# Attention's probabilities transposed in 32x32 blocks on VectorE and regrouped by DMA, in place of TensorE transposes

## The chip, the cores and the metric

The kernel runs on one core of one Trainium2 chip. The metric is the device time of one execution in microseconds (us), as the median of several runs. TensorE (PE, with its weight loads PEld), VectorE (DVE), ScalarE (ACT), GpSimd (POOL) and the DMA queue of SyncE (SP) run side by side, each through its own instructions in a fixed order, and wait for each other by semaphores.

## The reference

All of it is fp32. Three stages follow each other:

```
chunked attention: q, k, v (8 batches, 8 heads, 576, 64), chunks of 64
  s = (q_c @ k_c^T) / 8 ;  p = exp(s - max(s)) / (sum + 1e-9) ;  o = p @ v_c
  x = o as (4608 tokens, 512)
cos layer:   h = x @ w_in (512x2048) ;  y = (h * cos(h)) @ w_out (2048x512)
SoLU layer:  h2 = y @ w_in2 (512x1024) ;  z = h2 * softmax(h2)
             out = layernorm(z) * g_ln @ w_out2 (1024x512)
```

## The kernel before, in words

The large products are done as three matmuls on split operands (high by high, high by low, low by high), 128x512 each. Tokens go in 9 tiles of 512. The first part of the program is a row of 144 steps, 16 for each tile: step n does twelve matmuls `h` (`mm_in`, the first product, lines 533 to 535), ScalarE and VectorE make h*cos(h) out of it and split it into `gh` and `gl`, and two steps later twelve matmuls `y` (`mm_out`, lines 600 to 602) add it into the second product. The SoLU layer follows, tile by tile of 128 tokens (`h2` and `o`).

Attention is done in 20 units, numbered from 0. Units 0 to 3 hold 128 tokens each and run ahead of the steps. Units 4 and 5 hold 256 tokens, are loaded in natural order and have operands that step over 8 elements (`natural`). Units 6 to 19 hold 256 tokens as well (two units to a tile of 512); they are the 14 units that the change touches. The table `wide` spreads the work of such a unit over eight steps: q and k transposed in 32x32 blocks on VectorE (`att_tr`), 32 small matmuls 64x64 for the scores `sc` (`att_qk`), maximum, subtraction, exponential, sum and division (`att_max` to `att_mul`, tile `p`), then in step 5 `att_pt`: eight 128x128 transposes of `p` on TensorE into the PSUM tile `pt`. In step 6 `att_ptc` copies `pt` to SBUF on ScalarE (tile `ptb`), `att_pv` does 32 small matmuls with v (PSUM tile `x`), and in step 7 `att_x` splits `x` on ScalarE and VectorE into `xh` and `xl`, from which the `h` matmuls of that tile of 512 tokens read. The first step that reads both units of tile j is step 16j: step 32 for units 6 and 7, step 48 for units 8 and 9, and so on.

The PSUM tiles `sc`, `pt` and `x` of these units share one buffer (tag `a`), and `qt`, `kt`, `p`, `ptb` share two SBUF buffers (tag `t`, `work`). Many helpers show as line 105, so rows are told apart by tile.

A scheduler sets the order of each engine's instructions when the program is built: it takes what it believes ready, by priority of the place in the program. Calls through `pe`, `act`, `dve` are held to program order only ahead of the steps; within the steps matmuls of different tiles can be placed among each other. The chip then runs the order as it is. All loads and most stores are issued by SP, one after the other; a load or store whose condition isn't met holds back those behind it. There are eight DMA semaphores taken in turn, and a DMA waits for the one eight places before it.

Of the kernel before, what the change touches and what calls it, by code (L numbers as in the profile page):

```python
# [29 lines left out]
def kernel(  # L30
# [12 lines left out]
    nc = tc.nc  # L43
# [5 lines left out]
    CH = 64  # L49
# [107 lines left out]
    def wtile(dt, name, n=1024):  # L157
        return wp.tile([P, n], dt, tag="w", name=name)
# [103 lines left out]
    UNITS = [(2 * i, 2) for i in range(SUB)] + [(c, 4) for c in range(8, NT // CH, 4)]  # L262
    NU = len(UNITS)
    HU = H // 2


    NAT = SUB + 2
    GA = 8

    def small(i):  # L270
        return i < SUB

    def work(i, shape, tag, name):

        if small(i) or (i == SUB + 1 and tag != "t"):
            t = wtile(F32, name, 512 if small(i) else 1024)
        else:
            t = ap_.tile([P, 1024], F32, tag=tag, name=name, bufs=2 if tag == "t" else 1)
        letters = "abcde"[:len(shape)]
        sizes = {x: n for x, n in zip(letters, shape)}  # L280
        return t.rearrange(f"p ({' '.join(letters)}) -> p {' '.join(letters)}", **sizes)
# [17 lines left out]
    v0 = su.tile([P, HU, 2 * SUB, D], F32, name="v0")  # L299
# [96 lines left out]
    def natural(i, ap):  # L396
        return ap.rearrange("p (a g) -> p g a", a=GA) if SUB <= i < NAT else ap
# [58 lines left out]
    pt, ptb = {}, {}  # L456

    def att_pt(i):
        p = pr.pop(i)
        x = UNITS[i][1] // 2 * HU  # L460
        if small(i):
            t = ps_h.tile([P, x, P], F32, tag="h", name="pt")
        else:
            t = ps_a.tile([P, x, P], F32, tag="a", name="pt")
        for y in range(x):
            pe.transpose(out=t[:, y], in_=p[:, y].rearrange("p r k -> p (r k)"), identity=ident)
        pt[i] = t
# [8 lines left out]
    def att_pv(i):  # L476
        n = UNITS[i][1]

        t = (ps_y if small(i) else ps_a).tile([P, 2, 512], F32, tag="y" if small(i) else "a", name="x")
        a, b = vi.pop(i, None), ptb.pop(i)  # L480
        for y in range(n * HU // 2):
            for row in range(2):
                for col in range(2):
                    rs = slice(row * CH, (row + 1) * CH)
                    if small(i):
                        w, c = divmod(y, n)
                        u = 2 * w + col
                        m, p = v0[rs, u, UNITS[i][0] + c], b[rs, u, c * CH:(c + 1) * CH]
                    else:
                        u, cc = divmod(y, 2)  # L490
                        m, p = a[rs, cc, 2 * u + col], b[rs, cc * HU + u, col * CH:(col + 1) * CH]
                    pe.matmul(
                        out=t[col * CH:(col + 1) * CH, row, y * CH:(y + 1) * CH],
                        lhsT=m,
                        rhs=natural(i, p),
                        start=True,
                        stop=True,
                    )
        xps[i] = t[:, :, 0:n * HU // 2 * CH]
# [136 lines left out]
    if True:  # L636
# [23 lines left out]
        for c in range(4):  # L660
            sync.dma_start(
                out=gcol[32 * c:32 * (c + 1)],
                in_=g_ln.rearrange("(c q p) -> c p q", c=4, p=32)[c],
# [20 lines left out]
        att_mul(0)  # L684
        tok(2)
        att_pt(0)
        att_max(1)
        att_sub(1)
# [7 lines left out]
        att_mul(1)  # L696
        tok(3)
        att_pt(1)
        att_max(2)
        att_sub(2)  # L700
# [5 lines left out]
        att_sum(2)  # L706
        att_mul(2)
        att_pv(0)
        att_pt(2)
        att_max(3)  # L710
        att_sub(3)
        att_exp(3)
        att_ptc(2)
        att_pv(1)
        att_pv(2)
        att_sum(3)
        att_mul(3)
# [24 lines left out]
        def load_next_v(i):  # L742
# [3 lines left out]
        wide = (  # L746
            (0, "early", lambda i: att_tr(i, "q")), (1, "early", lambda i: att_tr(i, "k")),
            (1, "late", att_qk), (1, "late", load_next), (2, "early", att_max), (3, "early", att_sub),
            (3, "mid", att_exp), (4, "early", att_sum), (5, "early", att_mul), (5, "late", att_pt),
            (6, "early", att_ptc), (6, "late", att_pv), (6, "late", load_next_v), (7, "early", att_x),  # L750
        )
        tight = (
            (0, "early", lambda i: att_nat(i, "q")), (0, "early", lambda i: att_natc(i, "q")),
# [12 lines left out]
        for i in range(SUB, NU):  # L766
            j, o = divmod(UNITS[i][0] * CH, T)
# [111 lines left out]
        for n in range(NSTEP + LAG + 1):  # L879
# [20 lines left out]
            r = n - NB  # L900
# [8 lines left out]
            m, late_by = divmod(n - 40, 10)  # L909
# [69 lines left out]
```

## Time and profile before

| | |
|---|---|
| median of 3 runs | 1342.62 us (1342.1 to 1344.93) |
| profiled execution, its own time | 1340.4 us |
| span of the profiled execution | 1338.6 us |
| PE busy in the span | 1294.7 us (97%) |
| DVE busy | 928.0 us (69%) |
| ACT busy | 724.7 us (54%) |
| steps with attention of units 6 to 19 | about 170 to 820 us |
| mean granted TensorE clock | 0.992 |

Matmuls are pipelined: a row shows each from its start to its end, some 0.39 us for a 128x512 matmul, while the next starts 0.23 us after it. What an operation costs TensorE is read from the distance of starts.

### The profile page before, as it was taken

Reading aid. Unit: us, or ns where it says so; the run is one execution under the profiler, and the core shown is the slowest. Engines: PE = TensorE matmul, PEld = TensorE weight load, DVE = VectorE, ACT = ScalarE, POOL = GpSimd, SP = SyncE. Lnnn points to the kernel's source line nnn. Section 1 sums busy time; section 2 is a strip of 40 time slices with the busy share of each in tenths; the row PEclk is TensorE's granted clock in tenths of the full one; section 3 lists DMA queues with packets and bytes.
Section 4 is the critical chain, followed back from the end, with each engine's and each line's share of the span. In section 5 each row is a group of like instructions: output and inputs, shape, how many; then the busy total and the mean of one; then the engine's idle time right before and its main releaser. Section 6 shows DMA issues by size and latency. Waiting matters only on the chain.

```text
span 1338.6 us, 19864 instructions
## 1 busy us (share of the span) xinstructions
PE 1294.7 (97%) x7760; PEld 1035.8 (77%) x7760; DVE 928.0 (69%) x1362; ACT 724.7 (54%) x1065; POOL 23.1 (2%) x43
## 2 busy tenths in 40 slices
PE   5899999999999999999999999999799999999998
PEld 4566877888888888788888788887677888888877
DVE  4888987666786877877787776665676655666460
ACT  3877887666555556655564655455244343444241
POOL 0000000000000000000000000000000000000000
PEclk9899999999999999999999999999899999999999
DMA  8942342322431522332342300620623334333432
GB/s 244 208 101 71 118 111 64 60 78 53 111 94 29 148 50 62 97 77 57 86 94 50 117 10 14 222 79 1 190 86 102 87 87 126 87 87 79 95 73 69
DMA packets 212512, 122.98 MB, mean 92 GB/s; under 512 B 176065, under 2 KB 184257, under 8 KB 210881
## 3 DMA queue, kind: packets, MB, share of 16 engines
q1 hardware_dynamic: 212320, 121.57, 35.4%
q8 instruction: 61, 1.00, 0.3%
q14 instruction: 35, 0.28, 0.1%
q10 hardware_dynamic: 96, 0.13, 0.0%
HBM read 73.40 MB, written 29.36 MB: 77 GB/s over the span
## 4 chain that ended last, share of the span: by engine, by line
PE 83%; DVE 8%; ACT 5%; issue 1%; DMA 1%; POOL 0%; SPq 0%; DVEq 0%; ACTq 0%; POOLq 0%
PE h L533 9%; PE y L600 9%; PE y L602 9%; PE y L601 9%; PE h L535 9%; PE h L534 8%; PE o L865 5%; PE o L863 5%; PE o L864 5%; PE h L795 4%; PE h L794 4%; PE h L793 4%; DVE z L105 2%; PE x L105 2%; PE sc L105 1%
## 5 line engine op out<-in xcount | busy, mean ns | idle before, releaser
L533 PE MATMUL h<-xh,whi 128*128 128x512 f32 x576 | 232.9, 404 | 1.3 <-ACT xh L105 1.3
L534 PE MATMUL h<-xl,whi 128*128 128x512 f32 x576 | 225.7, 392 | 0.9 <-DVE xl L105 0.9
L535 PE MATMUL h<-xh,wlo 128*128 128x512 f32 x576 | 226.0, 392 | 0.1
L600 PE MATMUL y<-gh,whi 128*128 128x512 f32 x544 | 213.4, 396 | 3.9 <-ACT whi L105 2.0
L602 PE MATMUL y<-gh,wlo 128*128 128x512 f32 x544 | 214.9, 395 | 0.1
L601 PE MATMUL y<-gl,whi 128*128 128x512 f32 x544 | 214.9, 395 | 0.0
L562 ACT ACTIVATE r<-r 128x512 f32<-128x512 f32 x144 | 90.9, 631 | 177.1 <-DVE r L556 176.9
L570 DVE SCALAR_TENSOR_TENSOR hs<-r,hs 128x512 f32<-128x512 f32 x136 | 93.9, 690 | 96.2 <-ACT r L563 96.0
L105 DVE TENSOR_TENSOR gl<-hs,gh 128x512 fp32r<-128x512 f32 x136 | 93.7, 689 | 54.3 <-ACT gh L105 53.7
L105 ACT ACTIVATE gh<-hs 128x512 fp32r<-128x512 f32 x136 | 85.6, 630 | 83.2 <-DVE hs L570 76.7
L533 PEld LDWEIGHTS h<-xh,whi 128*128 128x128 f32 x576 | 108.6, 188 | 27.5 <-issue 1.6
L534 PEld LDWEIGHTS h<-xl,whi 128*128 128x128 f32 x576 | 108.7, 189 | 24.8 <-issue 1.7
L535 PEld LDWEIGHTS h<-xh,wlo 128*128 128x128 f32 x576 | 108.4, 188 | 24.4 <-issue 0.5
L600 PEld LDWEIGHTS y<-gh,whi 128*128 128x128 f32 x544 | 101.9, 188 | 29.7 <-ACT ye L610 3.5
L601 PEld LDWEIGHTS y<-gl,whi 128*128 128x128 f32 x544 | 102.1, 188 | 25.7 <-DVE gl L105 1.6
L793 PE MATMUL h<-whi,yh 128*128 128x512 f32 x288 | 113.2, 393 | 8.3 <-ACT yh L105 7.6
L602 PEld LDWEIGHTS y<-gh,wlo 128*128 128x128 f32 x544 | 102.1, 188 | 24.2 <-DVE wlo L105 0.5
L863 PE MATMUL o<-whi,lh 128*128 128x512 f32 x288 | 113.1, 393 | 3.9 <-ACT lh L105 3.9
L865 PE MATMUL o<-whi,ll 128*128 128x512 f32 x288 | 113.6, 394 | 3.1 <-DVE ll L105 2.7
L553 DVE SCALAR_TENSOR_TENSOR r<-kt,hs 128x512 f32<-128x512 int32 x144 | 99.4, 690 | 22.3 <-ACT kt L548 19.1
L794 PE MATMUL h<-wlo,yh 128*128 128x512 f32 x288 | 112.7, 391 | 0.0
L864 PE MATMUL o<-wlo,lh 128*128 128x512 f32 x288 | 112.6, 391 | 0.0
(93 smaller groups left out, 1941.2 us busy)
## 6 DMA issues: line engine op xcount, KB each, us to landing
lt<-bt SPq DMA_DIRECT2D x144, 128.0 KB
yd<-ye SPq DMA_DIRECT2D x22, 512.0 KB
yr<-yd SPq DMA_DIRECT2D x22, 512.0 KB
out<-os SPq DMA_DIRECT2D x142, 64.0 KB
vi<-in_v SPq DMA_DIRECT2D x64, 128.0 KB
qi<-in_q SPq DMA_DIRECT2D x224, 32.0 KB
ki<-in_k SPq DMA_DIRECT2D x224, 32.0 KB
st<-in_moe_w_in SPq DMA_DIRECT2D x10, 512.0 KB
```

Of the source, the lines that this page charges most:

```text
L105: ins = getattr(self.engine, name)(*args, **kwargs)
L533: nc.tensor.matmul(out=t, lhsT=wa, rhs=xh[j][:, kk, :], start=(kk == 0), stop=False)
L534: nc.tensor.matmul(out=t, lhsT=wa, rhs=xl[j][:, kk, :], start=False, stop=False)
L535: nc.tensor.matmul(out=t, lhsT=wb, rhs=xh[j][:, kk, :], start=False, stop=(kk == KD - 1))
L600: nc.tensor.matmul(out=o, lhsT=wa, rhs=a, start=head, stop=False)
L601: nc.tensor.matmul(out=o, lhsT=wa, rhs=b, start=False, stop=False)
L602: nc.tensor.matmul(out=o, lhsT=wb, rhs=a, start=False, stop=last)
L793: nc.tensor.matmul(out=ps[:, hh], lhsT=a[:, kk], rhs=whi, start=(kk == 0), stop=False)
L794: nc.tensor.matmul(out=ps[:, hh], lhsT=a[:, kk], rhs=wlo, start=False, stop=False)
L863: nc.tensor.matmul(out=o, lhsT=hi, rhs=whi, start=(f == 0), stop=False)
L864: nc.tensor.matmul(out=o, lhsT=hi, rhs=wlo, start=False, stop=False)
L865: nc.tensor.matmul(out=o, lhsT=lo, rhs=whi, start=False, stop=(f == NF2 - 1))
```

## The change

For units from `NAT` (6) on, `att_pt` issues one VectorE transpose of `p` in 32x32 blocks into a new tile `ptr`, and sixteen DMAs from SP, SBUF to SBUF, each 32 partitions of 256 elements (32 KB), which carry block (g, c) of `ptr` to partition group g of `ptb`. The TensorE transposes and the ScalarE copy of these units are gone (`att_ptc` stays for units 0 to 5). In `att_pv` the moving operand of these units is two runs of 32 elements, 256 elements apart, where it was 64 elements in a row. In `wide`, `att_mul` moves from step 5 early to step 4 late, with `att_pt` behind it; `att_pv` keeps step 6 late.

```diff
     def att_pt(i):
         p = pr.pop(i)
         x = UNITS[i][1] // 2 * HU
+        if i >= NAT:
+
+            t = work(i, (4, x, 32), "t", "ptr")
+            o = work(i, (4, x, 32), "t", "ptb")
+            tc.keep_in_program_order(
+                nc.vector.transpose(
+                    out=t.rearrange("p g x s -> p x g s"),
+                    in_=p.rearrange("p x r (h s) -> p x (r h) s", s=32),
+                )
+            )
+            for g in range(4):
+                for c in range(4):
+                    nc.sync.dma_start(
+                        out=o[32 * g:32 * (g + 1), c].rearrange("p x s -> p (x s)"),
+                        in_=t[32 * c:32 * (c + 1), g].rearrange("p x s -> p (x s)"),
+                    )
+            ptb[i] = o
+            return
         if small(i):
...
                     if small(i):
                         w, c = divmod(y, n)
                         u = 2 * w + col
-                        m, p = v0[rs, u, UNITS[i][0] + c], b[rs, u, c * CH:(c + 1) * CH]
+                        m, p = v0[rs, u, UNITS[i][0] + c], natural(i, b[rs, u, c * CH:(c + 1) * CH])
                     else:
                         u, cc = divmod(y, 2)
-                        m, p = a[rs, cc, 2 * u + col], b[rs, cc * HU + u, col * CH:(col + 1) * CH]
+                        m, x = a[rs, cc, 2 * u + col], cc * HU + u
+                        if i < NAT:
+                            p = natural(i, b[rs, x, col * CH:(col + 1) * CH])
+                        else:
+                            p = b[rs, 2 * col:2 * col + 2, x, :]
...
-                        rhs=natural(i, p),
+                        rhs=p,
...
-            (3, "mid", att_exp), (4, "early", att_sum), (5, "early", att_mul), (5, "late", att_pt),
-            (6, "early", att_ptc), (6, "late", att_pv), (6, "late", load_next_v), (7, "early", att_x),
+            (3, "mid", att_exp), (4, "early", att_sum), (4, "late", att_mul), (4, "late", att_pt),
+            (6, "late", att_pv), (6, "late", load_next_v), (7, "early", att_x),
```

The change moves instructions, since the scheduler orders anew. First place: TensorE at the product with v of unit 12, before. Its 32 matmuls (`x`) stand in one piece between the `y` of step 67 and the `h` of step 70.

```order
L601 MATMUL y_4447<-gl_4521,whi_1233 128x512
L602 MATMUL y_4447<-gh_4520,wlo_1234 128x512
L105 MATMUL x_4593<-ptb_4565,vi_4164 64x64 x32
L533 MATMUL h_4631<-xh_3734,whi_901 128x512
L534 MATMUL h_4631<-xl_3735,whi_901 128x512
```

The same unit now (its last two pieces; two more single matmuls stand further up, the first among the `h` of step 70, `h_4687`; `h_4732` is step 71):

```order
L555 MATMUL h_4732<-xh_3774,whi_901 128x512
L556 MATMUL h_4732<-xl_3775,whi_901 128x512
L105 MATMUL x_4649<-ptb_4553,vi_4212 64x64
L557 MATMUL h_4732<-xh_3774,wlo_902 128x512
L555 MATMUL h_4732<-xh_3774,whi_901 128x512
L556 MATMUL h_4732<-xl_3775,whi_901 128x512
L557 MATMUL h_4732<-xh_3774,wlo_902 128x512
L105 MATMUL x_4649<-ptb_4553,vi_4212 64x64 x29
```

The 32 matmuls are now in pieces of 1, 1, 1 and 29. Over units 6 to 19 the sizes are: 1, 1, 30 (unit 6); 1, 31 (unit 7); 1, 1, 1, 29 (units 8 to 13 and 15 to 17); 32 (units 14 and 19); 2, 1, 29 (unit 18), which is 46 pieces. Before, they were 4, 3, 2, 23 in unit 6, 5 and 27 in unit 18 and one piece in the other twelve, which is 18.

Second place: TensorE at the product with v of unit 7, now. `h_2445` is step 32, the first that reads what this unit makes (`xh_1953`, `xl_1954`); `h_2553` is step 33.

```order
L622 MATMUL y_2171<-gh_2463,whi_1820 128x512
L105 MATMUL x_2325<-ptb_2229,vi_1935 64x64
L623 MATMUL y_2171<-gl_2464,whi_1820 128x512
L624 MATMUL y_2171<-gh_2463,wlo_1821 128x512
L105 MATMUL x_2325<-ptb_2229,vi_1935 64x64 x31
L555 MATMUL h_2445<-xh_1953,whi_288 128x512
L555 MATMUL h_2553<-xh_1953,whi_288 128x512
L556 MATMUL h_2445<-xl_1954,whi_288 128x512
L557 MATMUL h_2445<-xh_1953,wlo_289 128x512
```

Before, two whole steps (48 matmuls 128x512) stood between the last `x` of unit 7 and the first `h` of step 32; now none does. In unit 17 five `y` matmuls stand between its last `x` and the first `h` of step 112; in the units 9, 11, 13 and 15 there are at least 12 large matmuls there.

Third place: VectorE behind the division of unit 12 (`p<-p,s`), before and then now. `gl_4435` and `gl_4483` are the split of step 65, `kt` and `r` belong to step 66.

```order
L105 TENSOR_TENSOR p_4429<-p_4429,s_4473 128x1024
L570 SCALAR_TENSOR_TENSOR hs_4391<-r_4394,hs_4391 128x512
L550 TENSOR_SCALAR kt_4440<-hs_4438 128x512
L553 SCALAR_TENSOR_TENSOR r_4441<-kt_4440,hs_4438 128x512
L105 TENSOR_TENSOR gl_4435<-hs_4391,gh_4434 128x512
```

```order
L105 TENSOR_TENSOR p_4477<-p_4477,s_4521 128x1024
L592 SCALAR_TENSOR_TENSOR hs_4439<-r_4442,hs_4439 128x512
L572 TENSOR_SCALAR kt_4488<-hs_4486 128x512
L466 STREAM_TRANSPOSE ptr_4552<-p_4477 128x8x4x32
L105 TENSOR_TENSOR gl_4483<-hs_4439,gh_4482 128x512
```

The new transpose stands two instructions behind the division and ahead of the split that the `y` of step 65 waits for; one `r` that stood ahead of that split is now behind it.

## Rows read from the trace of the kernel before

**Rows 1.** Page part 1: engine, busy us (share of the span), instructions.

```profile
PE 1294.7 (97%) x7760; PEld 1035.8 (77%) x7760; DVE 928.0 (69%) x1362; ACT 724.7 (54%) x1065; POOL 23.1 (2%) x43
```

**Rows 2.** Windows: us, busy of PE, PEld, DVE, ACT, POOL, PEclk, DMA share, GB/s.

```profile
440.00:480.00 40.00, 40.00 (x296) 32.48 (x295) 32.00 (x47) 23.50 (x34) 0.00 (x0) 1.00 0.46 124
```

**Rows 3.** Chain that ended last, in order of time: start us, us, what.

```profile
197.58 3.10 DMA vi<-in_v
...
448.42 1.09 PE sc L105 x64
...
471.81 0.87 PE pt L105 x8
...
478.24 1.09 PE x L105 x64
```

**Rows 4.** Groups by shape: busy us, mean ns, then idle before.

```profile
L105 PE MATMUL pt<-ident,p 128*128 128x128 f32 x144 | 20.4, 285 | 1.5 <-DVE p L105 1.5
...
L390 DVE STREAM_TRANSPOSE qt<-qi 128x1024 f32<-128x1024 f32 x14 | 17.3, 1237 | 0.0
...
L105 DVE TENSOR_TENSOR xl<-x,xh 128x1024 fp32r<-128x1024 f32 x16 | 19.6, 1224 | 3.9 <-ACT xh L105 3.9
...
L105 ACT ACTIVATE xh<-x 128x1024 fp32r<-128x1024 f32 x16 | 16.2, 1012 | 1.3 <-PE x L105 0.8 <-PE h L535 0.5
```

**Rows 5.** Timeline of PE around one whole product with v: start us, us, operation.

```profile
430.15 0.40 PE L602 MATMUL y<-gh,wlo 128*128 128x512 f32 x1
430.48 1.16 PE L105 MATMUL x<-ptb,vi 64*64 64x64 f32 x64
431.57 0.50 PE L533 MATMUL h<-xh,whi 128*128 128x512 f32 x1
431.90 0.40 PE L534 MATMUL h<-xl,whi 128*128 128x512 f32 x1
```

**Rows 6.** Timeline of PE, a piece of unit 18.

```profile
756.43 0.39 PE L535 MATMUL h<-xh,wlo 128*128 128x512 f32 x1
756.75 0.44 PE L105 MATMUL x<-ptb,vi 64*64 64x64 f32 x10
757.12 0.50 PE L600 MATMUL y<-gh,whi 128*128 128x512 f32 x1
757.46 0.39 PE L601 MATMUL y<-gl,whi 128*128 128x512 f32 x1
```

**Rows 7.** Timeline of PE, a piece of unit 6.

```profile
191.23 0.64 PE L600 MATMUL y<-gh,whi 128*128 128x512 f32 x2
191.80 0.33 PE L105 MATMUL x<-ptb,vi 64*64 64x64 f32 x4
192.06 0.50 PE L601 MATMUL y<-gl,whi 128*128 128x512 f32 x1
192.40 0.39 PE L602 MATMUL y<-gh,wlo 128*128 128x512 f32 x1
```

**Rows 8.** Timeline of PE, unit 4, whose moving operand steps over 8 elements.

```profile
69.55 2.09 PE L105 MATMUL x<-ptb,vi 64*64 64x64 f32 x64
71.58 0.50 PE L535 MATMUL h<-xh,wlo 128*128 128x512 f32 x1
```

**Rows 9.** Timeline of SP: sixteen DMAs of 32 partitions.

```profile
1074.74 10.04 SPq L847 DMA_DIRECT2D lt<-bt  x16
```

**Rows 10.** Timeline of DVE behind the division of units 12 and 13.

```profile
458.91 1.23 DVE L105 TENSOR_TENSOR p<-p,s 128x1024 f32<-128x1024 f32 x1
...
461.72 0.69 DVE L105 TENSOR_TENSOR gl<-hs,gh 128x512 fp32r<-128x512 f32 x1
...
510.39 0.68 DVE L105 TENSOR_TENSOR gl<-hs,gh 128x512 fp32r<-128x512 f32 x1
```

**Rows 11.** Timeline of PE: a wait for whi; first gl matmul behind unit 13.

```profile
215.44 0.50 PE L600 MATMUL y<-gh,whi 128*128 128x512 f32 x1 [1.99 <-ACT whi L105]
...
511.26 0.40 PE L601 MATMUL y<-gl,whi 128*128 128x512 f32 x1
```

## The prediction

> **What bounds the kernel now.** I read the page's busy times first: TensorE works 97% of the span, VectorE 69% [rows 1]. The windows then show where: in a stretch with units 11 and 12 TensorE is busy 40.00 of 40.00 us at a granted clock of 1.00, which is the upper of its two levels, 2.4 GHz, while VectorE has 8 us left and the DMA engines are under half busy [rows 2]. The chain that ended last is what the reader should look at next: in that stretch it stays on TensorE, and a unit's scores, its transposes (0.87 us) and its product with v lie on it one after the other [rows 3]. So here a microsecond taken off TensorE is a microsecond of the program, if nothing else comes late, and work added to VectorE or SP is free until TensorE waits for it. Durations of single matmuls mislead: a transpose lasts 285 ns on average [rows 4], but eight of them take 0.87 us of the chain.
>
> **What is removed.** Eight transposes of 14 units: 14 x 0.87 = 12.2 us off TensorE, all of it on the chain [rows 3]. The ScalarE copies of `pt` go too; they were hidden beside TensorE, so I give nothing for them.
> The Trainium skill's page "TensorE: Matmul & The Clock Gate", section "Part 4: PE-mode transpose", has a transpose at some 275 ns inside a kernel; the mean here agrees with that, but 14 x 8 x 0.275 would be 30.8 us by that figure, and the chain shows transposes pipelined, each starting some 0.1 us after the last. The row decides.
>
> **What the new order adds on TensorE.** The sum turns on the product with v, which the scheduler now cuts up: 46 pieces where there were 18, 28 more. What a cut costs is read from pieces that stand in the kernel before. A large matmul starts 0.23 us after the last (two together take 0.64 us, one 0.40 [rows 7]). A whole product (64 rows of the trace for 32 matmuls) stretches three starts of large matmuls from 0.46 to 431.90 - 430.15 = 1.75 us, so 1.29 us [rows 5]. A piece of 10 rows takes 757.46 - 756.43 - 0.46 = 0.57 us [rows 6]. The line through both is 13.3 ns for a row and 0.44 us for being a piece at all. A third piece tests it: 4 rows between large matmuls, 192.40 - 191.23 - 3 x 0.23 = 0.48 us, where the line gives 0.49. The fixed part is the gap on both sides (0.32 us to the first small matmul, 0.34 us from the first large one to the next) and the time in which one small matmul runs through alone. I take 0.43 us: 28 x 0.43 = 12.0 us. From below, a cut could cost 0.21 us, which is what is left if all of the whole product's 1.29 us but 64 x 17 ns (the 1.09 us of a product on the chain [rows 3]) is the piece's: 5.9 us. From above, the whole 0.48 us of the shortest piece: 13.4 us. The first four matmuls of a unit also wait for four DMA semaphores each; no TensorE row of before shows so many in one place, and I take nothing for it beside what the range holds.
>
> **What the new moving operand costs.** Two runs of 32 elements instead of 64 in a row: not in the trace. From below, nothing. From above, the product of unit 4, which steps over 8 elements: 71.58 - 69.55 = 2.03 us from its start to the next large matmul, against 1.09 in the whole product above, 0.94 us more [rows 5, 8], or 13 us in 14 units. I take nothing, since within a run the new operand is as contiguous as the one of 1.09 us.
> The Trainium skill's page "SBUF — State Buffer", section "Door 1: The DMA port swizzle", says that reads want at least two hits in each 16-byte line; a step of 8 fp32 gives one and runs of 32 give four. The rows agree for the step of 8; by that rule the new operand costs nothing either.
>
> **What the new waits cost.** The new chain from division to product, for unit 12: the division ends at 460.14, and three VectorE instructions fill the 1.58 us to the `gl` split at 461.72, 0.53 us each [rows 10]; now two of them stand ahead of the transpose, which runs 1.24 us, as the q and k transposes of the same size do [rows 4], to about 462.4. SP then issues sixteen DMAs; sixteen of the same partition count took 10.0 us [rows 9], so until 472.5, and if the last lands 3.1 us later, as a load on the chain did [rows 3], it is 475.6. The first small matmul now stands five steps and nine matmuls behind the scores: 448.42 + 1.2 + 129 x 0.23 = 479.3. Some 3.7 us remain, and the 29 come over 5 us later still. So the DMAs are hidden; if that cover were gone by 2 us in each unit, it would cost 28 us. What queues behind these DMAs on SP are the next unit's loads and w_in2/w_out2 loads, each wanted a unit (some 47 us) later.
> On VectorE the transpose stands ahead of the `gl` split of the next step. The tightest place I found is unit 13, where that split ended at 511.07 and its matmul started at 511.26, 0.19 us on [rows 10, 11]. The new transpose pushes the split by 1.24 us, and an `r` that moves behind it gives 0.53 back: a wait of 1.24 - 0.53 - 0.19 = 0.5 us there. For unit 9, the next tightest, I take 0.3: 0.8 us for all.
> The product of unit 7 now stands right before step 32, which reads its result. The next unit's k transpose (1.24 us) waits for the same product and is ahead of the `xl` split (1.22 us) on VectorE; the first `h` can start after `xh` (1.01 us) and the third wants `xl` [rows 4]. 1.24 + 1.22 + 0.1 less the 0.46 us of two `h`: 2.1 us of idle TensorE. In unit 17 five `y` and the first two `h` cover most: 0.6 us. Units 9, 11, 13 and 15 have 12 or more large matmuls (2.8 us) in between: nothing.
> In the other direction, the order around step 27 puts the preparation of a `w_out` pair ahead of unit 7's q and k transposes on VectorE; TensorE waited 1.99 us for that pair's `whi` [rows 11]. I count 1.5 of it as gone. The SoLU layer is ordered as before and follows TensorE; I give it nothing.
>
> **Sum.** -12.2 + 12.0 + 0.8 + 2.7 - 1.5 = +1.8 us, from 1340.4 us, the profiled execution's own time (1.8 us outside its span of 1338.6), to 1342.2. The median of the runs is 2.2 us above that execution, so I forecast 1344.4 us: the gain is spent by the cuts. What a measurement of this kernel can tell from no change is about 0.2%, 2.7 us: same is 1339.9 to 1345.3.
>
> **Rivals.**
> 1. The cuts are cheap (0.21 us) and the early waits vanish: 1342.6 - 12.2 + 5.9 = 1336 us, faster. For it: nothing is idle around the cuts, and pieces of one matmul are shorter than any in the rows. Against: three pieces of different length lie on one line. If the pieces cost nothing at all, it would be 1330 us.
> 2. DMAs come late: TensorE, in order, stands at the first small matmul of each unit with all `h` and `y` behind it. It decides from the point at which the last needed DMA lands over 3.7 us later than worked out, as when the load of 1 MB in unit 10 sits in the DMA engines ahead of them. At 1 to 2 us a unit: +14 to +28 on the sum, 1358 to 1372 us. Against: SP's pace and VectorE's place are rows; engines are under half busy.
> 3. The two-run operand pays the stepped price: +13, 1357 us. Against: only short runs have shown it.
>
> **How the numbers follow.** The forecast has 0.62, with an own range of 1340 to 1349 us for the pieces' and waits' bounds; of it 0.05 lies under 1339.9, 0.35 within, 0.22 above. Rival 1 has 0.17, of which 0.02 within; rival 2 has 0.12; rival 3 has 0.07; 0.02 is for other things. Faster 0.20, same 0.37, slower 0.43. The range runs from rival 1 to most of rival 3: 1335 to 1357 us.
>
> **What would show it.** Right: no `pt` rows from unit 6 on; starts of large matmuls 0.67 to 0.70 us apart around a single `x` instead of 0.23; a whole-TensorE wait of about 2 us for `xl` at step 32; idle before the small matmuls near zero. Rival 1: around single `x` less than 0.5 us. Rival 2: idle on `x` with the DMA of `ptb` as releaser. Rival 3: the 29 take 0.9 us more. I am wrong if the time is under 1336 with cuts at full price, or over 1350 with none of these waits.

## The result, and the profile after

The changed kernel takes 1361.16 us (median of 4 runs, 1359.84 to 1361.59), the kernel before 1342.42 us beside it: a ratio of 1.0134, with a 95% interval of 1.0116 to 1.0151. It is slower by some 18 us, above the range of the forecast. The profiled execution took 1361.1 us, with a span of 1359.3 us, so the two spans are 20.7 us apart.

The busy times of the page look almost as before [rows 1]; TensorE is even busier by 10.5 us, though 112 transposes are gone:

```profile
PE 1305.2 (96%) x7648; PEld 1031.8 (76%) x7648; DVE 941.5 (69%) x1376; ACT 712.8 (52%) x1051; POOL 23.1 (2%) x43
```

Windows say more (columns as in [rows 2]): the stretch that answers to [rows 2] is as full as before, while in those at 215 and 260 us TensorE waits, the one at 775 us stands right behind a wait (until 774.67, below), and in all three the granted clock (the last column but two) is far under 1.00.

```profile
215.00:220.00 5.00, 4.46 (x14) 3.50 (x14) 4.03 (x4) 0.63 (x2) 0.00 (x0) 0.66 0.37 76
...
260.00:265.00 5.00, 3.26 (x26) 2.20 (x19) 2.35 (x2) 1.28 (x2) 0.00 (x0) 0.80 0.87 259
...
440.00:480.00 40.00, 40.00 (x286) 32.09 (x286) 32.90 (x47) 23.17 (x33) 0.00 (x0) 1.00 0.40 99
...
775.00:780.00 5.00, 5.00 (x16) 3.98 (x15) 1.32 (x3) 1.84 (x3) 0.00 (x0) 0.66 0.61 216
```

The kernel before kept its clock in the window of its own wait for `whi`:

```profile
215.00:220.00 5.00, 4.50 (x18) 3.40 (x19) 3.90 (x5) 3.36 (x4) 0.00 (x0) 1.00 0.35 55
```

The cuts, in the timeline of TensorE (start us, us, operation). The first single matmul of unit 12 (two rows of the trace) stretches two starts of large matmuls to 488.83 - 487.93 = 0.90 us where 0.46 are due: 0.44 us. Over all 31 single ones the median is 0.46 us, and the pieces of 29 take 1.28 us.

```profile
487.93 0.39 PE L557 MATMUL h<-xh,wlo 128*128 128x512 f32 x1
488.24 0.33 PE L105 MATMUL x<-ptb,vi 64*64 64x64 f32 x2
488.50 0.50 PE L555 MATMUL h<-xh,whi 128*128 128x512 f32 x1
488.83 0.39 PE L556 MATMUL h<-xl,whi 128*128 128x512 f32 x1
```

A whole product with the new operand of two runs, unit 14: its first large matmul behind starts 1.10 us after it, against 1.09 us in [rows 5].

```profile
583.85 0.40 PE L624 MATMUL y<-gh,wlo 128*128 128x512 f32 x1
584.17 1.16 PE L105 MATMUL x<-ptb,vi 64*64 64x64 f32 x64
585.27 0.50 PE L555 MATMUL h<-xh,whi 128*128 128x512 f32 x1
585.61 0.39 PE L556 MATMUL h<-xl,whi 128*128 128x512 f32 x1
```

The three long waits of TensorE, same view, idle time and its releaser in brackets. Behind each the reader should look at the distances of starts: 0.43 us a matmul, where 0.23 is usual.

```profile
214.41 0.50 PE L622 MATMUL y<-gh,whi 128*128 128x512 f32 x1 [2.28 <-ACT whi L105]
...
215.67 0.80 PE L624 MATMUL y<-gh,wlo 128*128 128x512 f32 x1 [0.54 <-DVE wlo L105]
216.26 0.63 PE L622 MATMUL y<-gh,whi 128*128 128x512 f32 x1
216.69 0.63 PE L623 MATMUL y<-gl,whi 128*128 128x512 f32 x1
...
261.41 0.73 PE L555 MATMUL h<-xh,whi 128*128 128x512 f32 x2 [1.13 <-ACT xh L105]
262.74 0.60 PE L556 MATMUL h<-xl,whi 128*128 128x512 f32 x1 [0.60 <-DVE xl L105]
263.14 0.63 PE L557 MATMUL h<-xh,wlo 128*128 128x512 f32 x1
...
770.01 0.39 PE L557 MATMUL h<-xh,wlo 128*128 128x512 f32 x1
774.67 0.48 PE L622 MATMUL y<-gh,whi 128*128 128x512 f32 x1 [4.27 <-DVE ye L634]
...
775.37 0.63 PE L624 MATMUL y<-gh,wlo 128*128 128x512 f32 x1
775.80 0.63 PE L622 MATMUL y<-gh,whi 128*128 128x512 f32 x1
```

From the starts of all TensorE rows from 163 us to step 131 (where the changed kernel is 19.3 us behind) I made this account, in us; a large matmul counts 0.228.

| | forecast | trace |
|---|---|---|
| transposes removed | -12.2 | -12.3 (14 x 0.88) |
| 28 more pieces | +12.0 | +12.9 (0.46 each) |
| new waits for `gl`, `gh` | +0.8 | +3.6 |
| waits at steps 32 and 112 for `xh`, `xl` | +2.7 | +2.1 |
| wait for `whi`, `wlo` at 215 us | -1.5 | +0.8 |
| wait for `ye` at 774 us | none | +4.3 |
| matmuls at the lower clock level behind the three waits | none | +4.9 |
| the rest, in many small stretches | none | +3.0 |
| SoLU layer | none | +1.5 |

The lower-level term comes from the starts: 7 distances up to 218.74 us are 1.5 us longer than due, 9 up to 266.50 us 1.7, 10 up to 778.62 us 1.7.

For the row of 3.0 no run shows a cause. The row of the SoLU layer goes with the clock too: in that layer the changed kernel has three stretches at the lower level (from 966, 1000 and 1045 us on), the kernel before two (from 945 and 1300 us on), the last 2 us left aside. From step 131 to the end, the profiled execution of e7 below, with one such stretch, takes 493.8 us, the eight kernels with two take 495.8 to 497.0, and the four with three (the changed one, e1, e3, e8) 497.6 to 499.1.

So the cuts did cancel the gain, as forecast, and most of the loss stands where I had put +2 in waits: 10.8 us of waits, and 4.9 us at the lower clock behind three of them. The wait for `ye` shows how it arises. VectorE (start us, us, operation) is full there from 755 to 774.5 us: the transpose of unit 18, then, in between the steps' own work, the preparation of a weight pair of the SoLU layer (`z`, `st`), and only then `ye`, the copy that frees the PSUM buffer for which the next `y` waits.

```profile
763.18 1.24 DVE L466 STREAM_TRANSPOSE ptr<-p 128x1024 f32<-128x1024 f32 x1
...
767.32 1.22 DVE L105 SCALAR_TENSOR_TENSOR z<-st,z 128x1024 int32<-128x1024 int32 x1
...
768.79 1.22 DVE L105 CUSTOM_DVE_ANT_0 z<-st,z 128x2048 uint16<-128x2048 uint16 x1
...
771.25 1.41 DVE L122 SCALAR_TENSOR_TENSOR st<-z,gcol,st 128x512 fp32r<-128x512 f32 x2
...
773.30 1.22 DVE L634 TENSOR_SCALAR ye<-y 128x1024 f32<-128x1024 f32 x1
```

Before, the same pair's preparation began on ScalarE at 720.56 us, and VectorE was done with it almost 5 us ahead of `ye`:

```profile
747.60 1.41 DVE L122 SCALAR_TENSOR_TENSOR st<-z,gcol,st 128x512 fp32r<-128x512 f32 x2
...
753.97 1.22 DVE L612 TENSOR_SCALAR ye<-y 128x1024 f32<-128x1024 f32 x1
```

Why the pair is so late stands on SP's queue. Before, its four loads (`st`, line 224) are issued together at 699.78 us; this is SP before (start us, us from the first issue to the last):

```profile
699.78 1.86 SPq L224 DMA_DIRECT2D st<-in_moe_w_out  x4
718.38 3.73 SPq L105 DMA_DIRECT2D vi<-in_v  x4
```

and SP now, with two loads behind unit 17's sixteen DMAs and two behind the loads `vi` that follow them:

```profile
724.34 10.84 SPq L473 DMA_DIRECT2D ptb<-ptr  x16
735.22 1.05 SPq L224 DMA_DIRECT2D st<-in_moe_w_out  x2
745.79 3.12 SPq L105 DMA_DIRECT2D vi<-in_v  x4
748.95 1.09 SPq L224 DMA_DIRECT2D st<-in_moe_w_out  x2
```

Between the two halves SP does not issue at all: `vi` waits for the product with v of unit 17, which now ends at 745.8, and holds back the two loads behind it. The waits of SP from 715 to 760 us (us in total, times, longest):

```profile
SPq L105 <- PE x L105: 9.4, 1, 9.4
```

TensorE itself waits for no DMA of `ptb` in the changed kernel. In unit 12 the division ends at 469.05, the transpose starts at 469.91, the DMAs are issued from 472.66 to 484.59 us (11.9 us; sixteen took 10.0 in [rows 9]), and the first small matmul starts at 488.24 without idle.

### The profile page after: what moved, and what is told of

Same layout as the page of the kernel before. It is cut to its first block, busy times and chain, and to the rows that moved or that the text cites. A ratio compares the mean times of both kernels' runs of the same rounds, so it can differ in the third digit from the quotient of the medians.

```text
span 1359.3 us, 20014 instructions
## 1 busy us (share of the span) xinstructions
PE 1305.2 (96%) x7648; PEld 1031.8 (76%) x7648; DVE 941.5 (69%) x1376; ACT 712.8 (52%) x1051; POOL 23.1 (2%) x43
## 4 chain that ended last, share of the span: by engine, by line
PE 77%; DVE 12%; ACT 5%; DMA 2%; issue 1%; SPq 1%; POOL 0%; DVEq 0%; ACTq 0%; POOLq 0%
PE y L623 8%; PE y L624 8%; PE h L555 8%; PE h L557 8%; PE h L556 8%; PE y L622 8%; PE o L887 5%; PE o L885 5%; PE o L886 5%; PE h L817 4%; PE h L816 4%; PE h L815 4%; DVE z L105 3%; PE x L105 2%; SPq L105 1%
## 5 line engine op out<-in xcount | busy, mean ns | idle before, releaser
L562 ACT ACTIVATE hs<-h 128x512 f32<-128x512 f32 x144 | 85.1, 591 | 72.0 <-PE h L557 62.8
```

## The experiments

Theory: two things cost the time, the pieces and the place of SP's sixteen DMAs among the loads; the long waits follow from the second. Rivals: the DMAs' own landing, the table's earlier slots, GpSimd being no better a queue. Ratios are to the kernel before on the same chip; 0.1% is 1.34 us.

**e1: one piece.** The changed kernel with the DMAs of a unit issued last first.

```diff
-            for g in range(4):
-                for c in range(4):
+            for g in (3, 2, 1, 0):
+                for c in (3, 2, 1, 0):
```

> The sixteen DMAs of a unit are issued in the opposite order, so that the first small matmul with v needs the last of them; the product with v then stands in one piece in all 14 units (18 pieces fewer to 14, against 46), and little else moves. Theory A (pieces): a cut costs TensorE 0.46 us (0.35 around the small matmuls and 0.11 behind the next large one), 32 cuts go, so 1361.2 - 14.7 = 1346.5 us, with the waits at 214, 261 and 774 us still there. Theory B (the DMAs set the end of each unit, the pieces only fill time in which TensorE would wait for them): the time stays at 1358 to 1363 us and idle with a DMA as releaser appears ahead of the small matmuls.

Measured: 1347.32 us, ratio 1.0050 (1.0032 to 1.0067), 11 us less than the changed kernel by the two ratios. All products stand in one piece, and TensorE spends some 14.5 us less on them, as theory A had it; the waits grew by 3.3 us, one for `ye` to 6.03, with the same slow matmuls behind it. A single wait of 0.81 us has a DMA of `ptb` as releaser. Theory B falls.

```profile
764.28 0.77 PE L622 MATMUL y<-gh,whi 128*128 128x512 f32 x1 [6.03 <-DVE ye L634]
764.85 0.63 PE L623 MATMUL y<-gl,whi 128*128 128x512 f32 x1
```

**e2: the table alone.** The kernel before with

```diff
-            ... (5, "early", att_mul), (5, "late", att_pt),
+            ... (4, "late", att_mul), (4, "late", att_pt),
```

> The kernel before with only the table changed: division and TensorE transposes one slot earlier (step 4 late), everything else as it was. Theory A1 (the new waits come from the table's earlier slots): waits of several us at the first step of tile 2 and at the end of tile 6, 1348 us or more. Theory A2 (they come from the DMAs, which make the scheduler put the product with v and what follows it later): 1341 to 1344 us, as before.

Measured: 1341.45 us, ratio 1.0000 (0.9990 to 1.0011). The earlier slots cost nothing: A1 is out, and A2 is left for e3.

**e3: another queue.** As e1, with the DMAs issued by GpSimd.

```diff
-                    nc.sync.dma_start(
+                    nc.gpsimd.dma_start(
```

> As e1, and the sixteen DMAs are issued by GpSimd instead of SP, so that loads of weights and of the next unit no longer stand behind them; the scheduler then puts the product with v about where the kernel before has it. Theory A2: with one piece a unit and the old places the gain of 12.4 us is left, less 1 to 4 us for the transpose on VectorE: 1331 to 1335 us. Theory C (GpSimd takes over 1 us for a DMA, or slows VectorE while it works): the product waits for the DMAs, 0.5 us or more in most units, 1345 us or more.

Measured: 1335.16 us, ratio 0.9954 (0.9938 to 0.9970): faster than before, at the upper end of what theory A2 gave it. A weight pair's four loads are together on SP again:

```profile
695.53 1.86 SPq L224 DMA_DIRECT2D st<-in_moe_w_out  x4
```

The wait for `ye` is 0.95 us. GpSimd is not much faster an issuer: its sixteen DMAs for unit 12 take from 461.59 to 473.10 us, 0.50 us each with waits for earlier ones in between; over the 14 units the median is 8.6 us, against 10.6 us on SP in the changed kernel. For unit 17, whose DMAs stand next to the pair's loads, it is 10.6 against 10.8 us, so `ptr` is held no shorter there; what differs is the queue. Only unit 6 waits for its DMAs (1.59 us), so theory C falls.

```profile
461.59 3.95 POOL L473 DMA_DIRECT2D ptb<-ptr  x8 [40.62 <-DVE ptr L466]
467.30 0.50 POOL L473 DMA_DIRECT2D ptb<-ptr  x1 [1.76 <-DMA ptb<-ptr]
468.17 1.90 POOL L473 DMA_DIRECT2D ptb<-ptr  x3 [0.37 <-issue]
471.14 1.96 POOL L473 DMA_DIRECT2D ptb<-ptr  x4 [1.06 <-DMA ptb<-ptr]
```

The Trainium skill's page "DMA: Bandwidth & Descriptors", section "Issuing engine by pattern", gives simple copies to Sync and calls the path of SP and ScalarE generally faster than GpSimd's. By issue time GpSimd is a little faster here, and by the program's time the measurement decides for GpSimd, since nothing else waits behind it.

**e4: `ye` elsewhere.** As e1, the copy done by ScalarE.

```diff
-            if m == 0 or j < 2:
+            if m == 0 or j < 2 or j == 6:
```

> As e1, and the second half of the y tile that ends at step 111 is copied out by ScalarE instead of VectorE. Theory A: the wait of 4.27 us for that copy and the lowered clock behind it (nine matmuls at 0.43 instead of 0.23 us, 1.7 us) go: 6 us less than e1, about 1340.5 us. Rival: VectorE is behind there in any case, the next step's split is late instead, and no more than 2 us is saved.

Measured: 1344.83 us, ratio 1.0029 (1.0020 to 1.0039), 2.8 us less than e1: neither. The wait is 2.65 us, now for ScalarE, whose copy stands behind an instruction that waits 2.10 us for VectorE, and the matmuls behind it still go at the lower clock (starts 0.43 us apart).

**e5: the queue alone.** The changed kernel with GpSimd's queue, DMAs in the old order (the edit of e3 without that of e1).

> The changed kernel with nothing but the queue of the sixteen DMAs changed, GpSimd in place of SP, in their old order. The product with v then stands in 18 pieces, four more than in e3, and in the old places. Theory D (SP's queue is the cause of both losses: of the pieces, since the scheduler spreads the arrivals of slow DMAs, and of the new waits, since loads stand behind them): 1335.2 + 4 x 0.46 = 1337.0 us. Rival (the order of the DMAs is needed as well): near e1, 1345 us or more.

Measured: 1339.22 us, ratio 0.9977 (0.9967 to 0.9987), 3.1 us above e3. The queue alone brings the pieces from 46 to 18. Three waits for `ptb` of 1.4 to 1.5 us in the cut units 6 and 18, where e3 has one of 1.59, account for the rest above the expected 1.8. Theory D.

**e6: SP, from unit 8 on.** As e1; units 6 and 7 keep the old way.

```diff
-        if i >= NAT:
+        if i >= 8:
```

(and likewise for the copy and the operand).

> As e1 (SP, last DMA first), but units 6 and 7 keep their TensorE transposes and the ScalarE copy; the change begins at unit 8. Theory D1 (units 6 and 7 stand only seven steps apart, and the DMAs' 12 us in unit 6 push unit 7 up to step 32): e1 lost 3.9 us against before between steps 18 and 36, which go: 1347.3 - 3.9 = 1343.4 us, with the wait for ye near 760 us still there. Rival (the waits are not tied to these two units): 1347.3 + 1.8 = 1349 us.

Measured: 1345.70 us, ratio 1.0025 (1.0015 to 1.0035), 3.4 us less than e1. Between steps 18 and 36 it loses at most 0.1 us against before, where e1 loses 3.9: the loss comes with units 6 and 7, as D1 says. That SP's queue is needed for it is shown by e3, where unit 7's product stands at 240.6 us (259.5 in e1) and step 32 waits for neither `xh` nor `xl`; that it lies in the seven steps between the two units is not shown by itself. The wait for `ye` is unchanged, 6.03 us at 758.72.

**e7: GpSimd, from unit 8 on.** The edits of e3 and e6.

> As e3 (GpSimd's queue), with the change from unit 8 on. By the same theory e3 lost 1.3 us between steps 18 and 36, so 1335.2 - 1.3 = 1333.9 us, the fastest of all. Rival: nothing was lost there beside the two units' gain, 1335.2 + 1.8 = 1337 us.

Measured: 1333.42 us, ratio 0.9938 (0.9922 to 0.9953), 2.1 us less than e3, with intervals that overlap. The rival's 1.8 us above e3 (a ratio of 0.997) lies outside this one, and in the traces e3 loses 1.3 us against before between steps 18 and 36 and e7 none.

**e8: a load put back on SP.** As e3, with sixteen DMAs a unit of the same size on SP, into DRAM tiles (`spare`) that nothing reads.

```diff
+                    nc.sync.dma_start(
+                        out=spare[i, g, c],
+                        in_=t[32 * c:32 * (c + 1), g].rearrange("p x s -> p (x s)"),
+                    )
```

> As e3, and SP issues sixteen more DMAs a unit, of the same size, from ptr into a spare place in DRAM that nothing reads. Theory D (what holds up the loads behind them on SP, the preparation of w2 pairs among them, costs the time, not the landing of ptb): the preparation slides behind the transpose again and TensorE waits 3 us or more for ye near 750 us: 1339 to 1344 us. Rival (only the way to ptb matters, SP has room): 1335 to 1337 us.

Measured: 1352.30 us, ratio 1.0082 (1.0061 to 1.0102), 17 us above e3. The pair's loads slide from 695.53 to 731.44 us (some 11 of it is the kernel's own lag behind e3 by then), and the wait for `ye` is back:

```profile
718.66 7.59 SPq L481 DMA_DIRECT2D sp<-ptr  x16
728.29 3.10 SPq L105 DMA_DIRECT2D vi<-in_v  x4
731.44 2.03 SPq L224 DMA_DIRECT2D st<-in_moe_w_out  x4
```

```profile
767.38 0.77 PE L630 MATMUL y<-gh,whi 128*128 128x512 f32 x1 [3.60 <-DVE ye L642]
```

That is theory D in kind, but 17 us is twice the most that I gave it (9): there are another 3.60 us for `ye` at 571 us, and waits of 1.35 to 2.49 us ahead of the small matmuls with v in three places, two of them with a DMA of `ptb` as releaser and one with a spare copy. These stay unexplained; the doubled traffic and the longer hold on `ptr` are both candidates.

**e9: the pair out of the way, SP.** As e6, the last weight pair five steps later.

```diff
-                if late_by == 0:
+                if late_by == 0 and m < 7:
                     load_w2(*w2_order[m])
-                elif late_by == 3:
+                elif late_by == 3 and m < 7:
                     prep_w2(*w2_order[m])
+            if n == 110 + 5:
+                load_w2(*w2_order[7])
+            elif n == 110 + 8:
+                prep_w2(*w2_order[7])
```

> As e6 (SP, change from unit 8 on), and the last w2 pair is loaded and prepared five steps later, so that none of it stands ahead of the copy ye of tile 6. Theory E (e6's wait of 6.03 us and the lowered clock behind it, 7.6 us together, stand on that pair's preparation having slid onto VectorE right ahead of ye): the wait goes and 5 us or more are saved, a ratio to before of 0.999 or less. Rival F (it stands on unit 17 being late on SP's queue; with the pair gone, its product and the xl split stand there instead): TensorE waits 2 us or more for xl or ye at step 112, and the ratio stays at 1.001 or more.

Measured: 1340.48 us, ratio 0.9989 (0.9978 to 1.0000), 4.8 us less than e6, a little under the 5 of theory E. The wait for `ye` is gone, and the longest at step 112 is 0.59 us for `xl`: theory E, not rival F. A new one of 1.96 us for `ptb` stands at 825 us, in the last unit.

**e10: the same with GpSimd's queue.** The edits of e7 and e9.

> As e7 (GpSimd's queue, change from unit 8 on), with the last w2 pair five steps later. Theory E: e7's waits of 1.76 us for gh at 745 us and 0.93 us for ye at 752 us stand on the same pair and go: a ratio to before of 0.992, 2.5 us under e7. Rival: VectorE is as full there without the pair, no change from e7 (0.994).

Measured: 1330.71 us, ratio 0.9920 (0.9898 to 0.9942), as expected; this interval and that of e7 overlap, so the time alone doesn't exclude the rival's 0.994. The traces do: both waits are gone, and between steps 112 and 131 e10 gains 2.5 us on before where e7 loses 0.9. In steps with attention from unit 8 on no wait over 0.33 us is left. It is the fastest version, 10.8 us under before; its page, against [rows 1], shows TensorE with 10.5 us less work and GpSimd with 95 us more:

```profile
PE 1284.2 (97%) x7664; PEld 1025.9 (77%) x7664; DVE 939.9 (71%) x1374; ACT 712.4 (54%) x1053; POOL 118.2 (9%) x235
```

**e11: the pair later in the kernel before.** The edit of e9 on the kernel before.

> The kernel before with the last w2 pair loaded and prepared five steps later, nothing else. Theory E (that pair costs time only where the new chain has made VectorE full or SP late): no change, a ratio of 0.999 to 1.001. Rival (moving the pair helps any version, and e10's gain over e7 is not the new chain's): a ratio of 0.998 or less.

Measured: 1341.53 us, ratio 0.9998 (0.9988 to 1.0008). The pair costs nothing without the new chain; theory E.

## Why the prediction was wrong

- **What is removed** was right: -12.3 us for -12.2. So was the **price of a cut**, 0.46 us for 0.43, though a single small matmul is shorter than any piece of the rows; e1 shows it as the largest term that can be undone by itself. Rival 1 is out (its price, 1.29 us less 64 x 17 ns, is 0.20 and not 0.21 us).
- **The two-run operand** costs nothing (1.10 against 1.09 us); rival 3 is out. **Rival 2** in its form, TensorE standing at a small matmul, did not come either: that 1361 us lies in its band of 1358 to 1372 is luck. Slower had the largest chance, 0.43, but 0.19 of it lay on rivals 2 and 3, which did not come, and 0.22 on a loss of a few us.
- **The step that failed**: "What queues behind these DMAs on SP are the next unit's loads and w_in2/w_out2 loads, each wanted a unit (some 47 us) later." I looked at whether the loads are in time for TensorE, and put nothing in the sum for their being late. But VectorE has to prepare what they bring, in an order fixed when the program is built; that the scheduler goes by the time at which it believes a load has come is my reading, the order itself is in the traces. The pair's loads were issued 35 to 49 us later than before. Some 11 us of these are the kernel's own lag by then; units 16 and 17 put 10 to 11 us of DMAs each ahead of them, and the last two also stood behind SP's wait of 9.4 us for the product with v. The pair's preparation then came into the fullest stretch of VectorE, right ahead of `ye`: a wait of 4.27 us and 1.7 us at the lower clock, the largest single part of what the sum missed. e9 and e11 show the pair as the cause of that wait, e3 and e8 SP's queue as the cause of the pair's place.
- **"I count 1.5 of it as gone"** failed too: it rested on VectorE's order alone. ScalarE's first instruction of that pair starts at 205.72 us where it was at 206.12; TensorE, with less to do before, waits the longer for `whi`: 2.28 and 0.54 us for 1.99 [rows 11].
- **Step 32** was right in place and size, as waits go (1.73 us for 2.1). Its cause I had as an accident of order; e6 ties it to the change in units 6 and 7, and e3 to SP's queue. The 1.7 us of lower clock behind it were not in the sum.
- **`gl`** was undersized, 3.6 us for 0.8: I had checked two places. The longest waits, 1.04 us at 766 and 0.93 us at 188, do stand behind a new transpose; but 0.66 us at 579 stands behind the preparation of a weight pair and 0.52 us at 227 behind a unit's maximum and subtraction, so the new order of VectorE costs beside the transpose itself.
- **The clock** was not in the sum at all. Three waits of 1.7 to 4.3 us were followed by matmuls at the lower level, 4.9 us together, so that a wait of some us cost up to twice itself. Whether the clock falls is not set by the length of the wait alone: the same 1.99 us for `whi` leave it at 1.00 in the kernel before and in e10, and in e9 the window 217.5 to 220.5 us behind them has 0.50.
- **The signs** that I named could not tell this: no `pt` rows, a wait of about 2 us at step 32 and no idle before the small matmuls all came, and around a single `x` large matmuls start 0.57 us apart with 0.10 us more behind the next (0.67 in sum). None of them looks at what stands behind the DMAs on SP. What is left of the miss, 3.0 us in small stretches, stays open.

## What to carry to other kernels

DMAs added to a queue that also carries loads cost by what they stand ahead of, and in a kernel ordered by a scheduler also by where they push the work that uses those loads; read the queue and the order of every engine that prepares data, not only the one that bounds. Where arrivals are spread, let the first consumer need the last arrival, so that a run of small matmuls is not cut up. A queue on an idle engine, even one that issues hardly faster, can be worth more than the operation saved.

## What was new about the hardware

- A single 64x64 fp32 matmul between 128x512 ones costs 0.46 us (31 of them in the changed kernel), while 32 in a row cost 1.30 (unit 14).
- TensorE's granted clock stayed at 1.00 after a wait of 1.99 us in the kernel before [rows 11], and behind the same wait of 1.99 us in e9 it fell to 0.50 (217.5 to 220.5 us). In the changed kernel it fell to 0.66 in the window after waits of 2.28 and 0.54 us with one matmul pair between, and after one of 4.27 us: 1.2 in place of 2.4 GHz for 7 to 10 matmuls.
- GpSimd issued DMAs from SBUF to SBUF of 32 KB at 0.50 us each, and they landed 1.7 us (median, 7.7 at most) after the issue; VectorE's transposes kept their 1.24 us beside it (e3).
